# First layer of the first token tile's first column group in plain float32, with those weights' splits eight slots later

## The chip, the cores and the metric

The kernel runs on one core of a Trainium2 chip. The metric is the device time of one execution in microseconds (us). The kernel before took 508.42 us, the median of three runs (508.11 to 509.48).

## What is computed

Three blocks follow one another on 1536 tokens (2 batches of 768) with 512 features (8 heads of 64).

```python
# attention: local window of 16 keys each side, and 24 block summaries
k_sum = k.reshape(B, H, nb, 32, D).max(axis=3); v_sum = v.reshape(B, H, nb, 32, D).mean(axis=3)
scores_all = concat([where(mask_l, scale * q @ k.T, -1e9), scale * q @ k_sum.T + log(32)])
x = softmax(scores_all) @ concat([v, v_sum])          # 1536 x 512
# a two-layer block with 2048 hidden columns; w_in and w_out are float64
h = x @ w_in
g = where(h > 0, h, exp(min(h, 0)) - 1)
x = g @ w_out
# a routed block: 8 experts, argmax over x @ w_gate, relu(x @ w1[e]) @ w2[e], scaled by the gate
```

The change is in the second block and in its seam with the first.

## The kernel before, in words

The tokens are four tiles of 384 (`NT = 4`, `TT = 384`). The two-layer block runs over two groups of eight hidden column chunks of 128 (`NG = 2`, `FPG = 8`): for each group, for each tile t, for each chunk f, the first layer `mm1(t, f)` (line 387) makes `h` for 128 hidden columns and 384 tokens, the elu makes `g`, and the second layer `mm2(t, f)` (line 417) adds the chunk into three accumulators of 128 tokens.

**Precision.** Both layers work on split float32r values: a value is stored as a rounded copy and the rest (`x - rounded`), and a product is three matmuls (line 392). So `mm1` is 12 matmuls (4 chunks of 128 features times 3 passes). `xT[t]` holds both halves of the attention output: `act_o` (line 311, ScalarE) writes the rounded copy from PSUM, `dve_o` (line 317, VectorE) the rest; both read the PSUM bank "O".

**Weights.** `w_in` and `w_out` come as float64 words of 512 KB a chunk (`w_load`, 4 buffers). `w_conv` (line 359) makes float32 of one chunk with three VectorE instructions of 128x512 (lines 368, 372, 375). `w_split` (line 378) makes the two halves: a ScalarE copy (line 381) and a GpSimd subtraction (line 382). `i0` to `i7` are the chunks of `w_in`, `o0` to `o7` those of `w_out` of the first group. The weights of the second group are converted later and stored in HBM (`w_stash`), one per slot from slot 17 on. Splits are queued in `wpend` and done by `split_next`.

**Slots.** The order is written out by hand in one loop over slots `sl` (line 885); each engine runs its instructions in that order. Attention works in units of three query blocks, unit `u = sl` up to slot 17: scores `pe_s`, `dve_max` (line 272), `act_exp` (279), `norm` (lines 285, 286 on VectorE and 287 on GpSimd), `pe_t` (transposes, 294), `act_t`, `pe_o` (306), `act_o`. Units 0 to 7 make the first tile's x. From slot 18 on two units are done together in two slots. The two-layer block starts at slot `LAG = 9` with a running start: slot 8 has its own code (line 917) that does `mm1(0, 0)` and `mm1(0, 1)`, the first three feature chunks first and the last one when units 6 and 7 are done. Slot `9 + n` then does `mm1(0, n + 2)`, the elu of chunk n and `mm2(0, n - 1)`, up to n = 8. Slots 9 to 16 are called dense (line 1105); in them VectorE does `dve_max`, the elu's last step `elu_max` (line 404), one or two conversions interleaved with `norm`, and `dve_o`; GpSimd does the rest of `g` (`g_lo`, line 413), the splits and `norm`. From slot 17 on the second tile follows, chunk 0 first. `mm1` writes two PSUM banks in turn; a bank is free when `elu_max` has read it.

**Which weights when.** `corder` (line 834) converts, before the change, i0 in slots 5 and 6, i1 in 6 and 7, i2 in 7, o0 and i3 in 8, then o1 and i4 in 9, up to o4 and i7 in 12, o5 and o6 in 13 and o7 in 14. A split follows in the same slot (up to slot 8) or in the next.

Of the kernel before, what the change touches and what calls it, by code (L numbers as in the profile page):

```python
# [9 lines left out]
F32 = mybir.dt.float32  # L10
F32R = mybir.dt.float32r
BF16 = mybir.dt.bfloat16
I32 = mybir.dt.int32
U32 = mybir.dt.uint32
AF = mybir.ActivationFunctionType
ALU = mybir.AluOpType
# [4 lines left out]
P = 128  # L21
# [5 lines left out]
QB = 64  # L27
# [5 lines left out]
NCC = DM // P  # L33
# [4 lines left out]
TT = 384  # L38
# [11 lines left out]
def build(tc, cap, qT, kT, vT, vP, wi, wo, wg, wgT, wx, out):  # L50
# [6 lines left out]
    with ctx:  # L57
# [77 lines left out]
        mpool = px.enter_context(tc.tile_pool(name="mpool", bufs=2))  # L135

        xT = {}
        acc = {}
        W = {}

# [85 lines left out]
        def where(u):  # L226
            p, g = divmod(u, GPP)
            return p, p // NPAIR, p % NPAIR, g * GRP
# [81 lines left out]

        def act_o(u):
            p, t, pr, g0 = where(u)
            if pr == 0 and g0 == 0:
                xT[t] = xpool.tile([P, 2, NCC, TT], F32R, tag=f"xT{t}", name=f"xT{t}")
            nc.scalar.copy(xT[t][:, 0, pr, g0 * QB : (g0 + GRP) * QB], PS["o", u][:, 0 : GRP * QB])

        def dve_o(u):
            p, t, pr, g0 = where(u)
            q = slice(g0 * QB, (g0 + GRP) * QB)
            nc.vector.tensor_tensor(  # L320
                xT[t][:, 1, pr, q], PS.pop(("o", u))[:, 0 : GRP * QB], xT[t][:, 0, pr, q].bitcast(F32),
                op=ALU.subtract)
# [31 lines left out]
        def w_load(io, f):  # L354
            src = (wi if io == "i" else wo)[f].bitcast(U32)
            RW[io, f] = mpool.tile([P, 512, 2], U32, tag="raw", bufs=4, name=f"raw{io}{f}")
            nc.sync.dma_start(RW[io, f], src.rearrange("p (f two) -> p f two", two=2))

        def w_conv(which, parts=(0, 1, 2)):
            for part in parts:  # L360
                for io, f in which:
                    if part == 0:
                        raw = RW[io, f]
                        t = mpool.tile([P, 512], U32, tag="t1", bufs=T1, name=f"t1{io}{f}")
                        RW[io, f] = (raw[:, :, 0], raw[:, :, 1], t)
                    lo, hi, t = RW[io, f]
                    if part == 0:
                        nc.vector.tensor_scalar(
                            out=t, in0=hi, scalar1=3, scalar2=0x3FFFFFF8,
                            op0=ALU.logical_shift_left, op1=ALU.bitwise_and)  # L370
                    elif part == 1:
                        nc.vector.scalar_tensor_tensor(  # L372
                            out=t, in0=hi, scalar=0xC0000000, in1=t, op0=ALU.bitwise_and, op1=ALU.bitwise_or)
                    else:
                        nc.vector.scalar_tensor_tensor(  # L375
                            out=t, in0=lo, scalar=29, in1=t, op0=ALU.logical_shift_right, op1=ALU.bitwise_or)

        def w_split(io, f):
            src = RW.pop((io, f))[2].bitcast(F32)
            w = W[io, f] = wpool.tile([P, 2, 512], F32R, tag="W", name=f"W{io}{f}")  # L380
            nc.scalar.copy(w[:, 0], src)
            nc.gpsimd.tensor_tensor(w[:, 1], src, w[:, 0].bitcast(F32), op=ALU.subtract)  # L382

# [3 lines left out]
        def mm1(t, f, cs=range(NCC)):  # L387
            if cs[0] == 0:
                HP[t, f] = ph(f"h{t}_{f}")
            w = W["i", f]  # L390
            for c in cs:
                for n, (s, xs) in enumerate(((0, 0), (0, 1), (1, 0))):
                    nc.tensor.matmul(  # L393
                        HP[t, f][:, 0:TT], lhsT=w[:, s, c * P : (c + 1) * P], rhs=xT[t][:, xs, c, :],
                        start=c == 0 and n == 0, stop=c == NCC - 1 and n == 2)
# [228 lines left out]

        def alloc_expert(k):

            pl, tg = (wpool, "W") if k % 2 == 0 else (w2pool, "W2")
            EW[k] = [pl.tile([P, 2, 512], F32R, tag=tg, name=f"E{k}_{m}") for m in range(NCHUNK)]
            for i in range(k + 2, NE, 2):
                EW[i] = EW[k]  # L630

# [202 lines left out]
        corder = {}  # L834
        for f in range(NFC):
            if f < FPG:
                corder.setdefault(LAG - 4 + f, []).append(("i", f))
                corder.setdefault(LAG - 1 + f - (f > 5), []).insert(0, ("o", f))
            else:
                s0 = LAG + (NT - 1) * FPG + f % FPG  # L840
                corder.setdefault(s0, []).insert(0, ("i", f))
                corder.setdefault(s0 + 2, []).append(("o", f))
        order = [x for k_ in sorted(corder) for x in corder[k_]]
        nload = [0]


        later = order[2 * FPG :]
# [37 lines left out]
        for sl in range(total):  # L885
# [12 lines left out]
            if 0 <= n < FPG + 2:  # L898
                m1 = (0, 0, n + 2) if n + 2 < FPG else m1 if n >= FPG else None
                el = (0, 0, n) if 0 < n < FPG else el if n > FPG else None  # L900
                m2 = (0, 0, n - 1) if 0 <= n - 1 < FPG else None
            cv = list(corder.get(sl, ())) if sl >= LAG else []

            def conv_next():
                now = cv[:1]
# [11 lines left out]
            if sl == LAG - 1:  # L917

                pe_s(u)
                mm1(0, 0, range(NCC - 1))  # L920
                act_t(u - 2)
                w_split("i", 2)
                pe_o(u - 2)
                act_o(u - 2)
                w_conv([("o", 0)], (0, 1))
                dve_o(u - 2)
                pe_t(u - 1)
                mm1(0, 1, range(NCC - 1))
                w_conv([("o", 0)], (2,))
                w_prefetch()  # L930
                act_t(u - 1)
                pe_o(u - 1)
                w_split("o", 0)
                w_conv([("i", 3)], (0, 1))
                act_o(u - 1)
                dve_o(u - 1)
                mm1(0, 0, range(NCC - 1, NCC))
                mm1(0, 1, range(NCC - 1, NCC))
                w_conv([("i", 3)], (2,))
                w_prefetch()  # L940
                wpend.append(("i", 3))
                fin_va(p)
                load_vs(p)
                load_k(p + 2)
                dve_max(u)
                elu_exp(0, 0)
                elu_max(0, 0)
                act_exp(u)
                prep_k(p + 1)
                norm(u)  # L950
                g_hi(0, 0)
                g_lo(0, 0, nc.gpsimd)
                continue
# [182 lines left out]
            if dense:  # L1136
# [12 lines left out]
                w_conv(cv, (2,))  # L1149
                for x in cv:  # L1150
                    w_prefetch()
                wpend.extend(cv)
                cv = []
            if u < NU and sl % GPP == 0 and p + 1 < NPR:
                prep_k(p + 1)
            if u < NU and sl % GPP == 1 and p + 1 < NPR:
                if not dense:
                    prep_va(p + 1)
                if p + 2 < NPR:
                    load_vt(p + 2)  # L1160
            if sl == LAG - 3:
                w_conv([("i", 0)], (2,))
                w_prefetch()
                w_conv([("i", 1)], (0, 1))
            if sl == LAG - 2:
                w_conv([("i", 1)], (2,))
                w_prefetch()
            if sl < LAG and u - 2 in late:
                dve_o(u - 2)
            if u < NU and not dense:  # L1170
                norm(u)
            if sl in (LAG - 3, LAG - 2):
                w_split("i", sl - LAG + 3)
            if sl == LAG - 2:
                w_conv([("i", 2)])
                w_prefetch()
            if sl == LAG - 4:
                w_conv([("i", 0)], (0, 1))
            if sl >= LAG and u - 2 in late and not dense and u != NU:
                dve_o(u - 2)  # L1180
            if el and not dense:
# [286 lines left out]
```

## Time and profile before

| | |
|---|---|
| median of 3 runs | 508.42 us |
| the profiled execution | 508.64 us |
| its span | 506.9 us |
| TensorE matmuls busy | 472.0 us (93%), 3052 |
| weight loads busy | 406.9 us (80%) |
| VectorE busy | 325.6 us (64%) |
| ScalarE busy | 271.8 us (54%) |
| GpSimd busy | 189.3 us (37%) |
| granted TensorE clock, mean | 0.981 |

The profile is of one execution. PE is TensorE, PEld its weight loads, DVE VectorE, ACT ScalarE, POOL GpSimd, SP the engine that issues most DMAs. An instruction's duration includes what it waits for once it has started. Ends of matmuls are modelled, so a record is longer than the step to the next one. A clock of 1.00 is 2.4 GHz, 0.50 is 1.2 GHz.

### The profile page before, as it was taken

How to read it: one execution, taken by the hardware profiler on the slowest of the kernel's cores; microseconds unless marked ns; L12 is line 12 of the kernel's file. 1: busy time of each engine (PE TensorE's matmuls, PEld its weight loads, DVE VectorE, ACT ScalarE, POOL GpSimd, SP SyncE). 2: the span in 40 equal slices, each digit the busy share in tenths (PEclk: the TensorE clock that was granted, in tenths of full speed). 3: DMA queues.
4: the chain of work that ended last, by engine and by line, in shares of the span. 5: the costliest groups of instructions: out<-in, count | busy, mean ns of one | idle time of the engine just before them, and what ended most of it. 6: DMA issues, size and time to landing. Idle time of an engine off the chain costs nothing.

```text
span 506.9 us, 9236 instructions
## 1 busy us (share of the span) xinstructions
PE 472.0 (93%) x3052; PEld 406.9 (80%) x3052; DVE 325.6 (64%) x880; ACT 271.8 (54%) x681; POOL 189.3 (37%) x197
## 2 busy tenths in 40 slices
PE   7798798889999999999999999999998999999892
PEld 6586577678888889999999899888767989888672
DVE  4699999878877761111149889846686755556460
ACT  4755656666667646664333333334654865566550
POOL 4345575633333335883223233223335040030440
PEclk9988998999999999999999999999999999999997
DMA  8996656667777441439010010012645966458380
GB/s 237 283 255 185 191 162 189 214 207 245 227 230 219 126 142 46 125 118 345 37 62 2 0 63 0 2 63 88 200 129 151 345 211 222 135 164 278 105 292 15
DMA packets 45634, 79.97 MB, mean 158 GB/s; under 512 B 4604, under 2 KB 19196, under 8 KB 45552
## 3 DMA queue, kind: packets, MB, share of 16 engines
q1 hardware_dynamic: 43792, 73.83, 46.4%
q0 software_dynamic: 1760, 5.19, 3.4%
q8 instruction: 34, 0.56, 0.5%
q14 instruction: 48, 0.39, 0.2%
HBM read 65.29 MB, written 13.11 MB: 155 GB/s over the span
## 4 chain that ended last, share of the span: by engine, by line
PE 65%; DVE 15%; DMA 13%; issue 2%; ACT 2%; POOL 1%; SPq 0%; DVEq 0%; POOLq 0%
PE acc L426 23%; PE h L393 22%; DMA xgq<-x2d,gidx 10%; PE bh L750 6%; PE y L739 5%; DMA vt<-vT 2%; DVE t1i L375 2%; DVE t1i L372 2%; DVE t1o L375 1%; DMA xg<-x2d,gidx 1%; PE T L294 1%; DVE st L285 1%; DVE sc L272 1%; PE O L334 1%; DVE t1o L372 1%
## 5 line engine op out<-in xcount | busy, mean ns | idle before, releaser
L393 PE MATMUL h<-xT,Wi 128*128 128x384 f32 x768 | 152.8, 346 | 8.2 <-DVE e L404 6.6
L393 PEld LDWEIGHTS h<-xT,Wi 128*128 128x128 f32 x768 | 137.2, 192 | 16.5 <-DVE e L404 8.7
L426 PE MATMUL acc<-Wo,g 128*128 128x512 f32 x576 | 145.8, 397 | 1.0 <-POOL Wo L382 1.0
L413 POOL TENSOR_TENSOR g<-e,g 128x384 fp32r<-128x384 f32 x63 | 71.4, 1133 | 145.5 <-ACT g L409 129.9
L426 PEld LDWEIGHTS acc<-Wo,g 128*128 128x128 f32 x576 | 105.9, 188 | 21.7 <-POOL Wo L382 1.3
L404 DVE SCALAR_TENSOR_TENSOR e<-e,h 128x384 f32<-128x384 f32 x64 | 35.3, 551 | 77.3 <-ACT e L400 77.3
L399 ACT ACTIVATE e<-h 128x384 f32<-128x384 f32 x64 | 31.4, 491 | 65.4 <-PE h L393 61.8
L409 ACT CAST g<-e 128x384 fp32r<-128x384 f32 x64 | 32.8, 513 | 42.6 <-DVE e L404 42.6
L618 DVE TENSOR_TENSOR E<-rawq,E 128x512 fp32r<-128x512 f32 x70 | 46.7, 705 | 9.1 <-ACT E L608 8.0
L279 ACT ACTIVATE sc<-sc,st 128x120 f32<-128x120 f32 x96 | 36.8, 385 | 28.8 <-DVE st L272 28.6
L750 PE MATMUL bh<-xbq,E 128*128 128x256 f32 (+1 forms) x288 | 43.6, 303 | 2.7 <-ACT ysf L654 1.4
L608 ACT CAST E<-rawq 128x512 fp32r<-128x512 f32 x75 | 42.7, 617 | 6.2 <-DMA rawq<-wx 3.5
L750 PEld LDWEIGHTS bh<-xbq,E 128*128 128x128 f32 x288 | 41.3, 188 | 5.0 <-ACT ysf L654 1.6
L287 POOL TENSOR_TENSOR sc<-sc,st 128x360 f32<-128x360 f32 x32 | 29.6, 925 | 41.3 <-DVE st L286 20.1
L739 PE MATMUL y<-E,g 128*128 128x512 f32 x168 | 41.7, 393 | 0.0
L488 DVE CUSTOM_DVE_ANT_0 dot<-a,wgb 128x512 f32<-128x512 f32 x48 | 40.0, 887 | 0.0
L739 PEld LDWEIGHTS y<-E,g 128*128 128x128 f32 x168 | 30.6, 188 | 5.7
L400 ACT ACTIVATE e<-e 128x384 f32<-128x384 f32 x64 | 33.7, 526 | 2.0
L272 DVE CUSTOM_DVE_ANT_0 sc<-S,masks 128x120 f32<-128x120 f32 x96 | 21.5, 276 | 14.2 <-PE S L247 10.4
L758 DVE TENSOR_TENSOR g<-e,g 128x256 fp32r<-128x256 f32 (+1 forms) x24 | 11.3, 469 | 23.8 <-ACT g L757 23.6
L655 POOL DMA_INDIRECT out<-ys,sidx x6 | 6.3, 1053 | 47.4 <-ACT ys L654 46.0
L755 ACT ACTIVATE e<-bh 128x256 f32<-128x256 f32 (+1 forms) x24 | 10.1, 419 | 22.4 <-PE bh L750 22.4
(225 smaller groups left out, 634.5 us busy)
## 6 DMA issues: line engine op xcount, KB each, us to landing
rawq<-wx SPq DMA_DIRECT2D x88, 256.0 KB, 4.3
rawi<-wi SPq DMA_DIRECT2D x16, 512.0 KB, 5.0
rawo<-wo SPq DMA_DIRECT2D x16, 512.0 KB, 5.5
vw<-vP SPq DMA_DIRECT2D x16, 288.0 KB, 6.7
kt<-kT SPq DMA_DIRECT2D x8, 400.0 KB, 5.6
qt<-qT SPq DMA_DIRECT2D x16, 192.0 KB, 5.9
vt<-vT SPq DMA_DIRECT2D x8, 384.0 KB
out<-xg SPq DMA_DIRECT2D x12, 256.0 KB, 3.6
```

Source lines behind the costliest of these rows:

```text
L279: nc.scalar.activation(out=sc[:, gi], in_=sc[:, gi], func=AF.Exp, bias=st[:, 0, gi : gi + 1], scale=-1.0, accum_out=st[:, 1, gi : gi + 1])
L393: nc.tensor.matmul(HP[t, f][:, 0:TT], lhsT=w[:, s, c * P : (c + 1) * P], rhs=xT[t][:, xs, c, :], start=c == 0 and n == 0, stop=c == NCC - ...
L400: nc.scalar.activation(out=e, in_=e, func=AF.Relu, bias=1.0, scale=-1.0)
L404: nc.vector.scalar_tensor_tensor(out=e, in0=e, scalar=-1.0, in1=h[:, 0:TT], op0=ALU.mult, op1=ALU.max)
L409: nc.scalar.copy(gT[t, f][:, 0], EP[t, f])
L413: eng.tensor_tensor(g[:, 1], EP.pop((t, f)), g[:, 0].bitcast(F32), op=ALU.subtract)
L426: nc.tensor.matmul(accp[tb], lhsT=g[:, s, tb * P : (tb + 1) * P], rhs=w[:, ws], start=f % FPG == 0 and n == 0, stop=f % FPG == FPG - 1 and ...
L488: nc.vector.tensor_tensor_reduce(out=junk, in0=x2[t * BPT + tb], in1=WGB[e // 2][:, e % 2], scale=1.0, scalar=0.0, op0=ALU.mult, op1=ALU.a ...
L608: (nc.vector.tensor_copy if m in vec else nc.scalar.copy)(EW[k][m][:, 0], raw_of(k, m))
L618: (nc.gpsimd if m in pool else nc.vector).tensor_tensor(w[:, 1], raw, w[:, 0].bitcast(F32), op=ALU.subtract)
L739: nc.tensor.matmul(ys[b], lhsT=g[:, s, b * P : (b + 1) * P], rhs=w[:, ws], start=f == 0 and n == 0, stop=f == 7 and n == 2)
L750: nc.tensor.matmul(h[:, 0:nt], lhsT=EW[k][half * NCC + c][:, ws, fc * P : (fc + 1) * P], rhs=xb[:, s, c, 0:nt], start=n == 0, stop=n == 3 ...
```

## The change

For the first tile and the first group, `mm1` takes plain float32 operands: `act_o` writes the attention output as plain float32 into `X0`, `w_conv` writes the chunks i0 to i7 as plain float32 into `T0`, and `mm1(0, f)` for f below 8 is four plain float32 matmuls. `X0` and part of `T0` live in the buffer of the fourth tile's `xT`, the rest of `T0` in the homes of W i5 to i7. The split weights i0 to i7 are first needed by the second tile in slot 17; they are split from `T0`, queued one per slot in slots 16 to 23. `split_x0` makes the first tile's split xT, one feature chunk per slot in slots 20 to 23, for the second group. `dve_o` goes for the first tile. Each conversion of i0 to i7 runs about one slot later: i0 in slot 6, i1 in 7, i2 in 8 (with o0), then o1 and i3 in 9 up to o5 and i7 in 13, o6 in 14, o7 in 15. The split of o0 moves from slot 8 to slot 9. The split weights get one named buffer each instead of a pool of 16 in turn; expert 0's weights take the same buffers.

```diff
         def act_o(u):
             p, t, pr, g0 = where(u)
+            if t == 0:
+                if u == 0:
+                    x = xpool.tile([P, 2, NCC * TT], F32, tag=f"xT{NT - 1}", name="x0")
+                    X0.extend([x[:, 0].rearrange("p (c q) -> p c q", q=TT), x[:, 1].bitcast(U32)])
+                nc.scalar.copy(X0[0][:, pr, g0 * QB : (g0 + GRP) * QB], PS.pop(("o", u))[:, 0 : GRP * QB])
+                return
...
+        def split_x0(c):
+            if c == 0:
+                xT[0] = xpool.tile([P, 2, NCC, TT], F32R, tag="xT0", name="xT0")
+            x = X0[0][:, c]
+            nc.scalar.copy(xT[0][:, 0, c], x)
+            nc.vector.tensor_tensor(xT[0][:, 1, c], x, xT[0][:, 0, c].bitcast(F32), op=ALU.subtract)
+
         def dve_o(u):
             p, t, pr, g0 = where(u)
+            if t == 0:
+                return
...
+        def first_weights(f):
+            if not T0:
+                for a, last in ((0, 7), (2, 6), (4, 5)):
+                    w = wpool.tile([P, 2, 512], U32, tag=f"Wi{last}", bufs=1, name=f"T{a}")
+                    T0[a] = w[:, 0]
+                    T0[a + 1] = w[:, 1] if a < 4 else X0[1][:, 0:512]
+                T0[6], T0[7] = X0[1][:, 512:1024], X0[1][:, 1024:1536]
+            return T0[f]
...
-                        t = mpool.tile([P, 512], U32, tag="t1", bufs=T1, name=f"t1{io}{f}")
+                        if io == "i" and f < FPG:
+                            t = first_weights(f)
+                        else:
+                            t = mpool.tile([P, 512], U32, tag="t1", bufs=T1, name=f"t1{io}{f}")
...
-            w = W[io, f] = wpool.tile([P, 2, 512], F32R, tag="W", name=f"W{io}{f}")
+            w = W[io, f] = wpool.tile([P, 2, 512], F32R, tag=f"W{io}{f % FPG}", bufs=1, name=f"W{io}{f}")
...
         def mm1(t, f, cs=range(NCC)):
+            if t == 0 and f < FPG:
+                for c in cs:
+                    nc.tensor.matmul(
+                        HP[t, f][:, 0:TT], lhsT=T0[f][:, c * P : (c + 1) * P].bitcast(F32), rhs=X0[0][:, c],
+                        start=c == 0, stop=c == NCC - 1)
+                return
...
-                corder.setdefault(LAG - 4 + f, []).append(("i", f))
-                corder.setdefault(LAG - 1 + f - (f > 5), []).insert(0, ("o", f))
+                corder.setdefault(LAG - 3 + f, []).append(("i", f))
+                corder.setdefault(LAG - 1 + f, []).insert(0, ("o", f))
...
+            if FPG - 1 <= n < 2 * FPG - 1:
+                wpend.append(("i", n - FPG + 1))
+            if FPG + 3 <= n < FPG + 3 + NCC:
+                split_x0(n - FPG - 3)
...
                 mm1(0, 0, range(NCC - 1))
                 act_t(u - 2)
-                w_split("i", 2)
                 pe_o(u - 2)
                 act_o(u - 2)
-                w_conv([("o", 0)], (0, 1))
-                dve_o(u - 2)
+                w_conv([("i", 2)], (0, 1))
                 pe_t(u - 1)
                 mm1(0, 1, range(NCC - 1))
+                w_conv([("i", 2)], (2,))
+                w_prefetch()
+                w_conv([("o", 0)], (0, 1))
+                act_t(u - 1)
+                pe_o(u - 1)
+                act_o(u - 1)
                 w_conv([("o", 0)], (2,))
                 w_prefetch()
-                act_t(u - 1)
-                pe_o(u - 1)
-                w_split("o", 0)
-                w_conv([("i", 3)], (0, 1))
-                act_o(u - 1)
-                dve_o(u - 1)
+                wpend.append(("o", 0))
                 mm1(0, 0, range(NCC - 1, NCC))
                 mm1(0, 1, range(NCC - 1, NCC))
...
-                wpend.extend(cv)
+                    if x[0] == "o":
+                        wpend.append(x)
...
             if sl in (LAG - 3, LAG - 2):
-                w_split("i", sl - LAG + 3)
+                w_conv([("i", sl - LAG + 3)])
+                w_prefetch()
```

## Rows read from the trace of the kernel before

**Rows 1.** The page, chain that ended last, shares of the span by engine:

```profile
PE 65%; DVE 15%; DMA 13%; issue 2%; ACT 2%; POOL 1%; SPq 0%; DVEq 0%; POOLq 0%
```

**Rows 2.** Busy us (instructions) of each engine by stretch; clock, DMA share, GB/s last:

```profile
42.00:92.00 50.00, 41.98 (x300) 34.08 (x300) 48.86 (x110) 29.52 (x92) 31.52 (x24) 0.91 0.60 177
40.70:44.10 3.40, 3.35 (x18) 2.55 (x17) 2.90 (x10) 2.08 (x9) 1.05 (x1) 0.50 0.61 172
110.00:345.00 235.00, 234.73 (x1491) 208.59 (x1490) 138.69 (x403) 119.44 (x292) 90.50 (x82) 1.00 0.36 114
119.10:130.06 10.96, 10.96 (x102) 9.56 (x98) 9.73 (x29) 6.89 (x23) 3.86 (x4) 1.00 0.85 292
```

**Rows 3.** Groups of instructions, whole span: busy us, mean ns | idle before, releasers:

```profile
L393 PE MATMUL h<-xT,Wi 128*128 128x384 f32 x768 | 152.8, 346 | 8.2 <-DVE e L404 6.6 <-ACT xT L315 1.6
L426 PE MATMUL acc<-Wo,g 128*128 128x512 f32 x576 | 145.8, 397 | 1.0 <-POOL Wo L382 1.0
L258 PE MATMUL S<-kw,qt 64*64 64x120 f32 x216 | 16.0, 284 | 0.4 <-DVE st L272 0.3
L404 DVE SCALAR_TENSOR_TENSOR e<-e,h 128x384 f32<-128x384 f32 x64 | 35.3, 551 | 77.3 <-ACT e L400 77.3
```

**Rows 4.** VectorE in order of time, slot 11: start us, us, instruction:

```profile
59.61 0.27 DVE L272 CUSTOM_DVE_ANT_0 sc<-S,masks 128x120 f32<-128x120 f32 x1
...
61.67 0.68 DVE L372 SCALAR_TENSOR_TENSOR t1o<-rawo,t1o 128x512 uint32<-128x512 uint32 x1
62.27 1.50 DVE L372 SCALAR_TENSOR_TENSOR t1i<-rawi,t1i 128x512 uint32<-128x512 uint32 x1
63.69 1.24 DVE L285 TENSOR_SCALAR st<-st 128x3 f32<-128x3 f32 x1
...
65.06 1.62 DVE L375 SCALAR_TENSOR_TENSOR t1o<-rawo,t1o 128x512 uint32<-128x512 uint32 x1
66.61 1.27 DVE L375 SCALAR_TENSOR_TENSOR t1i<-rawi,t1i 128x512 uint32<-128x512 uint32 x1
67.80 0.27 DVE L272 CUSTOM_DVE_ANT_0 sc<-S,masks 128x120 f32<-128x120 f32 x1
```

**Rows 5.** GpSimd in order of time, slot 11, [idle before <- releaser]:

```profile
61.91 1.31 POOL L413 TENSOR_TENSOR g<-e,g 128x384 fp32r<-128x384 f32 x1 [2.92 <-issue]
63.18 1.72 POOL L382 TENSOR_TENSOR Wo<-t1o,Wo 128x512 fp32r<-128x512 f32 x1
64.86 1.27 POOL L382 TENSOR_TENSOR Wi<-t1i,Wi 128x512 fp32r<-128x512 f32 x1
66.09 1.24 POOL L287 TENSOR_TENSOR sc<-sc,st 128x360 f32<-128x360 f32 x1
```

**Rows 6.** TensorE in order of time, slot 8:

```profile
33.44 1.86 PE L393 MATMUL h<-xT,Wi 128*128 128x384 f32 x9
...
38.29 0.57 PE L306 MATMUL O<-pT,vw 120*64 120x64 f32 x12 [0.46 <-DVE xT L320]
40.48 2.43 PE L393 MATMUL h<-xT,Wi 128*128 128x384 f32 x6 [1.62 <-ACT xT L315]
```

**Rows 7.** TensorE in order of time, from slot 11 to slot 12:

```profile
64.55 0.50 PE L294 MATMUL T<-ident,sc 128*120 128x128 f32 x3
64.98 0.83 PE L258 MATMUL S<-kw,qt 64*64 64x120 f32 x12
...
69.01 2.35 PE L393 MATMUL h<-xT,Wi 128*128 128x384 f32 x12 [0.42 <-DVE e L404]
```

**Rows 8.** GpSimd in order of time, slots 14 and 15:

```profile
87.95 2.94 POOL L382 TENSOR_TENSOR Wo<-t1o,Wo 128x512 fp32r<-128x512 f32 x2
...
93.97 1.00 POOL L413 TENSOR_TENSOR g<-e,g 128x384 fp32r<-128x384 f32 x1 [2.32 <-issue]
```

**Rows 9.** VectorE in order of time, first scores of slot 15:

```profile
91.67 0.27 DVE L272 CUSTOM_DVE_ANT_0 sc<-S,masks 128x120 f32<-128x120 f32 x1
```

**Rows 10.** TensorE in order of time, first group of the second tile, slot 17:

```profile
101.37 2.27 PE L393 MATMUL h<-xT,Wi 128*128 128x384 f32 x12
```

More of the change, by code (lines that the diff above doesn't have):

```diff
@@ L137, in build @@
         xT = {}
+        X0 = []
+        T0 = {}
         acc = {}
@@ L625, in alloc_expert @@
         def alloc_expert(k):
-            pl, tg = (wpool, "W") if k % 2 == 0 else (w2pool, "W2")
-            EW[k] = [pl.tile([P, 2, 512], F32R, tag=tg, name=f"E{k}_{m}") for m in range(NCHUNK)]
+            if k % 2 == 0:
+                EW[k] = [
+                    wpool.tile([P, 2, 512], F32R, tag=f"W{io}{f}", bufs=1, name=f"E{k}_{m}")
+                    for m, (io, f) in enumerate(splits)]
+            else:
+                EW[k] = [w2pool.tile([P, 2, 512], F32R, tag="W2", name=f"E{k}_{m}") for m in range(NCHUNK)]
             for i in range(k + 2, NE, 2):
@@ L842, in build @@
                 corder.setdefault(s0 + 2, []).append(("o", f))
+        corder[LAG - 1].reverse()
         order = [x for k_ in sorted(corder) for x in corder[k_]]
         nload = [0]
+        splits = [("i", 0), ("i", 1)]
+        for f in range(2, FPG + 2):
+            splits += [x for x in (("i", f), ("o", f - 2)) if x[1] < FPG]
         later = order[2 * FPG :]
@@ L921, in build @@
                 act_t(u - 2)
-                w_split("i", 2)
                 pe_o(u - 2)
                 act_o(u - 2)
-                w_conv([("o", 0)], (0, 1))
-                dve_o(u - 2)
+                w_conv([("i", 2)], (0, 1))
                 pe_t(u - 1)
                 mm1(0, 1, range(NCC - 1))
+                w_conv([("i", 2)], (2,))
[4 more added lines that the diff above has]
+                act_o(u - 1)
                 w_conv([("o", 0)], (2,))
                 w_prefetch()
-                act_t(u - 1)
-                pe_o(u - 1)
-                w_split("o", 0)
-                w_conv([("i", 3)], (0, 1))
-                act_o(u - 1)
-                dve_o(u - 1)
+                wpend.append(("o", 0))
                 mm1(0, 0, range(NCC - 1, NCC))
                 mm1(0, 1, range(NCC - 1, NCC))
-                w_conv([("i", 3)], (2,))
-                w_prefetch()
-                wpend.append(("i", 3))
                 fin_va(p)
@@ L1160, in build @@
                     load_vt(p + 2)
[L1161 to L1167, printed above, removed]
             if sl < LAG and u - 2 in late:
@@ L1172, in build @@
             if sl in (LAG - 3, LAG - 2):
-                w_split("i", sl - LAG + 3)
-            if sl == LAG - 2:
-                w_conv([("i", 2)])
+                w_conv([("i", sl - LAG + 3)])
                 w_prefetch()
-            if sl == LAG - 4:
-                w_conv([("i", 0)], (0, 1))
             if sl >= LAG and u - 2 in late and not dense and u != NU:
```

## The prediction

> **What bounds the kernel now.** I read the chain that ended last first. It is 65% TensorE and 15% VectorE [rows 1], so the question is where each of the two rules. The busy time by stretch answers it [rows 2]: from 110 to 345 us TensorE is busy for 234.73 of 235.00 us, and whatever is gained before 110 us is kept only if TensorE reaches that stretch earlier. From 42 to 92 us it is the other way round: VectorE is busy 48.86 of 50.00 us, TensorE 41.98, and the clock granted to TensorE is 0.91 there, 0.50 (1.2 GHz) from 40.7 to 44.1 us: part of the time TensorE runs at half clock, and that costs little while VectorE is late. The groups of instructions say the same from TensorE's side [rows 3]: of 8.2 us that the matmuls of the first layer waited in all, 6.6 were for `e` of line 404, the VectorE step that frees their PSUM bank.
>
> One slot of that stretch shows why VectorE is late. Slot 11 runs from the first score row at 59.61 us to the next slot's at 67.80, 8.19 us [rows 4]. The same instruction on the same 128x512 tile (L372) takes 0.68 us and then 1.50; L285, which has three columns, takes 1.24. GpSimd's rows lie exactly beside them [rows 5]: L372 ends when `g` (L413) has ended, L285 ends with the Wo subtraction, L375 follows the end of the Wi subtraction, the last L375 that of L287. The two engines take turns, whole instruction by whole instruction: 1.27 us of this chain is the Wi subtraction.
>
> **The change, part by part.** The profiled execution took 508.64 us with a span of 506.9, 1.7 us around it; the median of the runs shown is 508.42, 0.2 less. Slots are numbered as in the loop.
>
> *Plain float32 matmuls.* A column group of the first tile had 12 float32r matmuls of 384 columns; it gets 4 plain ones. The trace has no plain product of 128x128 by 384. Plain products stand in it as two records each (L258 has 6 calls a slot and 12 records), with a mean of 284 ns for 120 columns; float32r has 346 for 384 and 397 for 512 [rows 3]. That is 0.40 ns a column, so 120 columns of float32r would have 346 - 264 x 0.40 = 240 ns; the plain record has 44 more, hence 0.77 ns a column. Nine float32r matmuls last 1.86 us at full clock [rows 6], 0.346 of it the last: eight steps of 0.19 us, 0.04 over their columns; twelve are 2.2 to 2.3. Eight plain records then cost 8 x (384 x 0.77 + 35 ns) = 2.6 us: 0.4 more per group, 3.2 for eight. Ends: 1.5 us if a plain record streams like float32r (8 x 0.19), 3.5 if the twelve records of L258 that last 0.83 us [rows 7] are two heads side by side (1.15 ns a column). I take 2.6, between them and from the recorded durations. It is covered in slots 10 to 13 only while VectorE is slower; uncovered it is the full 0.4.
>
> *Slot 8.* Before, the two first groups cannot finish until VectorE has emptied the output bank (a wait of 0.46 us) and ScalarE, which first stood behind a weight split, has stored the last xT (1.62 us); so the last column block starts at 40.48 us, at half clock, and ends at 42.91 [rows 6]. After, ScalarE alone empties the bank, no split stands in ScalarE's queue, and T0 needs only VectorE's three steps. From the start at 33.44: 6 records of 0.33, the output and transposes of about 0.95 us (from 35.2 to 36.0 with fill), 6 records, the last output and its copy 1.0, 4 records: 33.4 + 2.0 + 1.0 + 2.0 + 1.0 + 1.35 = 40.75 us. The first exp waits for the first of these two groups alone; its PSUM bank and the scores of slot 8 follow about 1.7 us earlier than now. VectorE has one weight conversion less before slot 9 (i3 moves into it) and no dve_o, so it isn't late. Gain 1.7 us, 0 if VectorE is late after all, 2.5 if not even that wait is left.
>
> *Slot 9.* o0's split takes the place of i3's on ScalarE and GpSimd: nothing.
>
> *Slots 10 to 13.* Each loses one Wi subtraction and one ScalarE copy. In slot 11, after the Wo subtraction (64.90 us), L285 and L286 run as now, then L375 at once (0.6) instead of after 66.13; L287 waits until that L375 ends (65.6), runs 0.8, and the second L375 0.5: 66.85 instead of 67.80. So 1.0 us, less than the 1.27 removed, since L287's turn is now waited for in the open. Four slots: 4.0 us. Bounds: 0 (L287 just takes the place) and 1.3 x 4 = 5.1. TensorE then has 4.04 us of other work between two first-layer groups (64.55 to 69.01, less the wait of 0.42) [rows 7] and 2.6 of its own, 6.65 of 7.2: still covered, and with so little idle time the half-clock stretches should go.
>
> *Slot 14.* It converted o7 beside two splits (2.94 us on GpSimd [rows 8]); now o6 beside one (half of that). L287 comes 1.3 us earlier and is out of the way of the slot's last VectorE copies: 0.6 us, between 0 and 1.3.
>
> *Slots 15 to 17 give back.* Now TensorE goes through them with hardly a wait: slot 15 begins at 91.67 on VectorE and the second tile's first group starts at 101.37, 9.7 us later [rows 9, 10]. After, slot 15 also converts o7 and slot 16 splits o7 and i0, and second-layer step f of the first tile waits for Wo f. In slot 15 GpSimd starts g 2.3 us after the slot's begin, as now (93.97 [rows 8]); g (1.0), a turn of L372 (0.6) and Wo6 (1.3) end at 5.2, and after the last turn of L375 VectorE closes the slot at 5.6. In slot 16 scores and elu (1.1), the exps and g's copy (1.6) put g at 8.3 to 9.3, Wo7 ends at 10.6, its nine matmuls take 2.2, and the first group of tile 1 starts at 12.8; Wi0 (11.9) is in time. Loss 3.1 us; 0 if GpSimd finds room beside VectorE's scores, 4.5 if Wi0 comes first.
>
> *Slots 17 to 23.* Seven more Wi splits and four split_x0 (a copy of 0.5 us and a subtraction of about 0.55 each, after L404's 551 ns for 384 columns [rows 3]) lie under the full TensorE; nothing, with the price in the third rival. Loads: the order of the raw loads shifts by one slot, each prefetch still two slots ahead of its use; SyncE's queue may be held some 2 us longer by the first one, ahead of q and v loads that are used two slots later: nothing.
>
> Sum: -1.7 - 4.0 - 0.6 + 3.1 = -3.2 us. 508.64 - 3.2 = 505.4, on the median's scale 505.2; I say 505.3.
>
> **The rivals.** (a) *The tail of the first tile gives nothing back*: Wo6 and Wo7 fit beside the scores, whose rows (0.27 us) aren't slowed beside GpSimd's end of L287 [rows 4, 5]. Against it: two GpSimd instructions more than now stand ahead of the second layer. Time: -6.3, 502.1.
>
> (b) *The turn is taken by the next one*: L287 or g holds VectorE as long as the Wi subtraction did, and slots 10 to 13 keep 8.2 us each. For it: every VectorE step from 62.27 on stands behind some GpSimd row [rows 4, 5]; against it, L287 is 0.8 us alone and was waited for already. Time: +0.8, 509.2.
>
> (c) *The moved subtractions come back in slots 18 to 23* (the slower side). VectorE is busy 9.73 of 10.96 us in a pair of slots there [rows 2], 1.23 idle. Two Wi subtractions of 1.27 may hold it 2.54 us, two split_x0 another 1.1. It decides once the added time passes the 1.23: 1.3 us in the first pair, 2.4 in each of the next two, 6.1 in all, 511.3. Against it: GpSimd is busy only 3.86 us of the pair, so that gaps are there, and scores that read PSUM take no turn. The Trainium skill speaks for this rival (SBUF — State Buffer, section "SBUF: two separate sides"): the port pair of the two engines is an exclusive lock that the first to start holds for its whole instruction, so a subtraction that is moved takes its hold along. The trace agrees on the hold: L285's 1.24 us [rows 4]; what it costs where TensorE rules no row shows.
>
> (d) *The plain matmuls cost 3.5 us*: 4.04 + 3.5 = 7.54 a slot, 0.3 over VectorE's 7.2 four times, and 1.8 more in slot 8. Time: +3.0 on the forecast, 508.3.
>
> **How the numbers follow.** My sum 0.52, (a) 0.15, (b) 0.12, (c) 0.13, (d) 0.08. About 0.3%, 1.5 us, is what a measurement here can tell from no change. Faster than 506.9 are nearly all of the sum's cases (0.49) and (a): 0.64. Within 0.3% lie (b), most of (d), and the sum's upper edge: 0.21. Slower: (c) and a worse (b): 0.15. The range leaves out the far half of (c) and the edge of (a): 501.8 to 509.3; the sum's own is 503.5 to 507.
>
> **What would show it.** Right: the first scores of slot 9 1.7 us earlier; slots 10 to 13 of 7.2 us, L285 and one L375 without a wait for Wi; eight records of L393 in about 2.6 us; the clock at full from 41 to 92 us; the second tile's first group at about 98 us, with waits of TensorE for Wo just before it; TensorE full from there. Wrong: slots of 8 us; a group of 3.5 us; waits for `e` of line 404 between 110 and 140 us.

## The result, and the profile after

The changed kernel takes 514.17 us, the median of five runs (510.33 to 516.87), against 508.42 for the kernel before in the same session (506.82 to 509.48). The ratio is 1.0104, 95% interval 1.0068 to 1.014: slower, and outside the range that was given. The profiled execution is the one of 514.17 us, with a span of 512.5, 5.6 more than before, and a mean granted clock of 0.988.

The first view is the busy time by stretch of the changed kernel. Columns: stretch, length, then busy us and instructions of PE, PEld, DVE, ACT and POOL, clock, DMA share, GB/s.

```profile
42.00:92.00 50.00, 44.58 (x308) 29.33 (x306) 47.67 (x112) 30.93 (x99) 27.20 (x21) 1.00 0.69 197
117.36:144.61 27.25, 23.09 (x200) 19.35 (x197) 24.21 (x62) 18.14 (x54) 13.31 (x13) 1.00 0.73 223
144.61:166.37 21.76, 21.76 (x197) 18.89 (x195) 16.93 (x57) 15.21 (x47) 7.81 (x9) 1.00 0.73 207
110.00:345.00 235.00, 230.84 (x1459) 204.73 (x1458) 142.54 (x400) 120.22 (x291) 96.00 (x85) 1.00 0.36 112
```

From 42 to 92 us it went as forecast: TensorE is busier than before (44.58 us against 41.98) and the clock is at 1.00, where it was 0.91 [rows 2]. But the stretch from 110 to 345 us, which TensorE filled before (234.73 of 235.00 us), now has 4.16 us of idle time, and all of it lies in slots 20 to 23: 27.25 us long, TensorE busy 23.09. The same four slots of the kernel before:

```profile
119.10:141.01 21.91, 21.91 (x198) 19.11 (x194) 17.98 (x56) 14.64 (x46) 7.89 (x9) 1.00 0.82 260
```

They are 5.34 us longer: 4.16 us of it is TensorE's idle time, the rest is busy time, mostly of runs that are now broken in two (the scores of a pair, 0.85 us before, are 0.42 and 0.83 us), whose ends are modelled. VectorE's busy time in them has grown by 6.23 us (17.98 to 24.21), GpSimd's by 5.42. Slots 24 to 27 take 21.76 us, as before.

The groups of instructions, as in [rows 3]: the plain product has its own line (L421), which stands twice because its tiles' buffers have different names. No first-layer matmul in split values (L428, second tile on) waits for anything. The scores of the paired units (L249) do.

```profile
L428 PE MATMUL h<-xT,Wi 128*128 128x384 f32 x672 | 129.8, 339 | 0.0
L421 PE MATMUL h<-x,T 128*128 128x384 f32 x40 | 14.4, 499 | 2.9 <-DVE e L439 2.5 <-ACT x L319 0.4
L421 PE MATMUL h<-x 128*128 128x384 f32 x24 | 8.5, 499 | 1.7 <-DVE e L439 1.7
L249 PE MATMUL S<-kw,qt 64*64 64x120 f32 x168 | 7.1, 273 | 2.4 <-DVE e L439 2.4
```

TensorE in slot 8, as in [rows 6]: six records for each of the first two groups, then the last column block of both at 41.31 us, ended at 42.87.

```profile
35.29 2.20 PE L421 MATMUL h<-x,T 128*128 128x384 f32 x6
...
38.30 2.10 PE L421 MATMUL h<-x,T 128*128 128x384 f32 x6
40.33 0.57 PE L308 MATMUL O<-pT,vw 120*64 120x64 f32 x12
41.31 1.56 PE L421 MATMUL h<-x,T 128*128 128x384 f32 x4 [0.42 <-ACT x L319]
...
43.95 2.85 PE L421 MATMUL h<-x,T 128*128 128x384 f32 x8 [0.32 <-DVE e L439]
```

VectorE and then GpSimd in slot 11, as in [rows 4, 5]: the slot lasts from 66.11 to 73.47 us, 7.36 instead of 8.19. After the turn of the Wo subtraction (L287, 1.23 us) the first L404 runs in 0.66, and no Wi subtraction stands before L289.

```profile
66.11 0.27 DVE L274 CUSTOM_DVE_ANT_0 sc<-S,masks 128x120 f32<-128x120 f32 x1
...
70.19 1.23 DVE L287 TENSOR_SCALAR st<-st 128x3 f32<-128x3 f32 x1
...
71.55 0.66 DVE L404 SCALAR_TENSOR_TENSOR t1o<-rawo,t1o 128x512 uint32<-128x512 uint32 x1
72.13 1.28 DVE L404 SCALAR_TENSOR_TENSOR x<-rawi,x 128x512 uint32<-128x512 uint32 x1
...
73.47 0.27 DVE L274 CUSTOM_DVE_ANT_0 sc<-S,masks 128x120 f32<-128x120 f32 x1
```

```profile
68.42 1.30 POOL L448 TENSOR_TENSOR g<-e,g 128x384 fp32r<-128x384 f32 x1 [2.78 <-issue]
69.68 1.71 POOL L411 TENSOR_TENSOR Wo<-t1o,Wo 128x512 fp32r<-128x512 f32 x1
71.80 1.06 POOL L289 TENSOR_TENSOR sc<-sc,st 128x360 f32<-128x360 f32 x1 [0.41 <-PE O L308]
```

TensorE at the end of the first tile, slots 16 and 17: a wait of 0.93 us for Wo6, one of 1.53 for the transposed scores of unit 15 (L300 on ScalarE), and the second tile's first group at 99.63.

```profile
92.21 2.11 PE L461 MATMUL acc<-Wo,g 128*128 128x512 f32 x8 [0.93 <-POOL Wo L411]
...
96.94 0.57 PE L308 MATMUL O<-pT,vw 120*64 120x64 f32 x12 [1.53 <-ACT pT L300]
97.44 2.35 PE L461 MATMUL acc<-Wo,g 128*128 128x512 f32 x9
99.63 0.69 PE L428 MATMUL h<-xT,Wi 128*128 128x384 f32 x3
```

The loss itself, TensorE from slot 20 to 22: in each pair of slots it waits once for the bank of the scores (0.88 and 0.80 us, L249 waiting for `e`) and once for ScalarE's copy pT (1.24, and 1.25 in the second pair).

```profile
118.65 0.83 PE L249 MATMUL S<-kw,qt 64*64 64x120 f32 x20 [0.88 <-DVE e L439]
...
127.64 0.52 PE L296 MATMUL T<-ident,sc 128*120 128x128 f32 x3 [1.24 <-ACT pT L300]
...
132.23 0.83 PE L249 MATMUL S<-kw,qt 64*64 64x120 f32 x20 [0.80 <-DVE e L439]
```

Why `e` is late stands in VectorE's rows from slot 19 to the begin of slot 20, beside GpSimd's Wi subtraction:

```profile
113.43 1.32 DVE L200 COPY kw<-ks 128x144 f32<-128x144 f32 x1
...
117.58 0.55 DVE L330 TENSOR_TENSOR xT<-x,xT 128x384 fp32r<-128x384 f32 x1
118.05 0.55 DVE L439 SCALAR_TENSOR_TENSOR e<-e,h 128x384 f32<-128x384 f32 x1
```

```profile
113.35 1.32 POOL L411 TENSOR_TENSOR Wi<-T,Wi 128x512 fp32r<-128x512 f32 x1
```

and the same two VectorE steps of the kernel before:

```profile
114.90 0.22 DVE L198 COPY kw<-ks 128x144 f32<-128x144 f32 x1
...
117.95 0.55 DVE L404 SCALAR_TENSOR_TENSOR e<-e,h 128x384 f32<-128x384 f32 x1
```

Slot 20 begins at 117.36 us after and at 119.10 before. So `e` starts 1.15 us before the slot's begin in the kernel before, and 0.69 after it in the changed one: 1.84 us later. Of this the copy that waits out the Wi subtraction makes 1.10 (1.32 for 0.22) and the new subtraction of split_x0 (L330) 0.5; the rest was there when the copy started. The first four of the 24 score records run at once; the next need the PSUM bank "S1", which `h` of the step before holds until L439 has read it.

The wait for pT comes by two ways. On VectorE a subtraction of split_x0 stands ahead of the next `e`; it takes 1.15 us beside GpSimd's L289 (123.70 to 124.76 us), where the one at 117.58 took 0.55. ScalarE's copy of `g` has to wait for that `e`, 1.57 us instead of 0.85 before. Behind it stand three more copies, Wi, kw and pT, of which Wi is new (0.52 us to the next one). The fourth, of split_x0, stands behind pT and costs nothing here: the next pT waits for TensorE anyway (0.28 us).

```profile
124.02 1.15 DVE L330 TENSOR_TENSOR xT<-x,xT 128x384 fp32r<-128x384 f32 x1
125.09 0.54 DVE L439 SCALAR_TENSOR_TENSOR e<-e,h 128x384 f32<-128x384 f32 x1
```

```profile
125.67 0.52 ACT L444 CAST g<-e 128x384 fp32r<-128x384 f32 x1 [1.57 <-DVE e L439]
126.09 0.61 ACT L410 CAST Wi<-x 128x512 fp32r<-128x512 f32 x1
126.61 0.51 ACT L197 COPY kw<-kt 128x384 f32<-128x384 f32 x1
127.02 0.47 ACT L300 COPY pT<-T 120x384 f32<-120x384 f32 x1
127.39 0.51 ACT L329 CAST xT<-x 128x384 fp32r<-128x384 f32 x1
128.19 0.48 ACT L300 COPY pT<-T 120x384 f32<-120x384 f32 x1 [0.28 <-PE T L296]
```

The copy of `g` in the kernel before, in the same place:

```profile
125.03 0.51 ACT L409 CAST g<-e 128x384 fp32r<-128x384 f32 x1 [0.85 <-DVE e L404]
```

### The profile page after: what moved, and what is told of

Same layout as the page of the kernel before. It is cut to its first block, busy times and chain, and to the rows that moved or that the text cites. A ratio compares the mean times of both kernels' runs of the same rounds, so it can differ in the third digit from the quotient of the medians.

```text
span 512.5 us, 9156 instructions
## 1 busy us (share of the span) xinstructions
PE 473.5 (92%) x3020; PEld 398.3 (78%) x3020; DVE 325.8 (64%) x876; ACT 272.8 (53%) x685; POOL 190.0 (37%) x197
## 5 line engine op out<-in xcount | busy, mean ns | idle before, releaser
L428 PE MATMUL h<-xT,Wi 128*128 128x384 f32 x672 | 129.8, 339 | 0.0
L428 PEld LDWEIGHTS h<-xT,Wi 128*128 128x128 f32 x672 | 118.0, 188 | 5.4 <-issue 1.5
L439 DVE SCALAR_TENSOR_TENSOR e<-e,h 128x384 f32<-128x384 f32 x64 | 35.3, 551 | 78.4 <-ACT e L435 78.4
L653 DVE TENSOR_TENSOR E<-rawq,E 128x512 fp32r<-128x512 f32 x70 | 48.2, 727 | 12.3 <-ACT E L643 11.5
L289 POOL TENSOR_TENSOR sc<-sc,st 128x360 f32<-128x360 f32 x32 | 29.5, 922 | 45.0 <-DVE st L288 32.8
L300 ACT COPY pT<-T 120x384 f32<-120x384 f32 x32 | 15.3, 478 | 14.3 <-PE T L296 12.6
```

Source lines behind the costliest of these rows:

```text
L428: nc.tensor.matmul(HP[t, f][:, 0:TT], lhsT=w[:, s, c * P : (c + 1) * P], rhs=xT[t][:, xs, c, :], start=c == 0 and n == 0, stop=c == NCC - ...
L439: nc.vector.scalar_tensor_tensor(out=e, in0=e, scalar=-1.0, in1=h[:, 0:TT], op0=ALU.mult, op1=ALU.max)
L653: (nc.gpsimd if m in pool else nc.vector).tensor_tensor(w[:, 1], raw, w[:, 0].bitcast(F32), op=ALU.subtract)
```

## The experiments

Runs of one session share the runs of the kernel before; ratios are to those. Times of stretches are read from TensorE's rows of each profile.

**Both kernels once more.**

> The changed kernel once more, unedited. Theory M (the moved subtractions and split_x0 come back in slots 18 to 23): TensorE's waits of about 5.3 us between its first group of tile 1 (slot 17) and slot 24 repeat to within 0.3 us, since they are made by the order of instructions. Rival R (the extra time comes from before 42 us, where the profile had a half-clock stretch of 6.8 us instead of 3.4 and a vt load 0.57 us later): the start of mm1(0,0), 35.29 us in the first profile against 33.44, is what varies from run to run, and the time goes with it.

Changed kernel: 513.94 us, before 509.83, ratio 1.0086 [1.0055, 1.0116]. The loss is there again; slots 20 to 23 took 26.13 us in this execution. The time up to the first first-layer group, 1.9 us longer in the first profile, is 0.1 shorter than before in this one. In the twelve profiles of changed versions that group starts anywhere from 31.46 to 38.03 us (33.44 and 34.03 in the two of the kernel before), so those 1.9 us aren't shown to be an effect of the change. From the second tile's first group to slot 20 this execution took 19.27 us instead of 17.72, with a stretch at half clock from 105 to 108 us (0.53); four of the twelve profiles have such a loss there, and why is not known.

> The kernel before, unedited, for a second profile. M: slots 20 to 23 take 21.9 us from the scores of slot 18's pair to those of slot 22's as in its first profile, the stretch from the last large expert to the first transposes of the small one (472 to 477 us) 4.3 us; the first 25 us vary by a few us from run to run, as they did between the profiles of the changed kernels (25.3 to 28.7 us). If instead the stretch at 472 us takes 6 to 7.5 us here as well, the 1.6 to 3.2 us that every changed kernel lost there have nothing to do with the change.

508.85 against 510.41, 0.9979 [0.9943, 1.0015]. Slots 20 to 23 took 21.91 us here too, to the hundredth.

**split_x0 moved out of slots 20 to 23**, to slots 24 and 25.

```diff
-            if FPG + 3 <= n < FPG + 3 + NCC:
-                split_x0(n - FPG - 3)
+            if n in (2 * FPG - 1, 2 * FPG):
+                for c in range(2):
+                    split_x0(2 * (n - 2 * FPG + 1) + c)
```

> split_x0 two chunks each in slots 24 and 25 instead of one each in slots 20 to 23. M: the waits of TensorE in slots 20 to 23 (5.3 us in the profile of the change) shrink to about 2.2, since 0.47 and 1.07 us of split_x0 stand directly ahead of line 404's step twice each; 3 us faster than the changed kernel, some 511. R: no change, 514.

512.39 us, 1.0048 [1.0019, 1.0077]. Slots 20 to 23: 23.37 us, 1.46 over the kernel before, with only the Wi splits in them. Slots 24 to 27: 23.22 instead of 21.76. Without split_x0 2.8 to 3.9 us of the loss are gone there, and in its new place, ahead of `elu_max` again, it costs 1.5 us. The copy L200 still takes 1.31 us beside the Wi subtraction.

**The Wi split behind prep_k and act_t**, in slots 19, 21 and 23.

```diff
-                split_next()
+                if even or n >= 2 * FPG:
+                    split_next()
...
                     act_t(a)
+                    if n < 2 * FPG:
+                        split_next()
```

> In slots 19, 21 and 23 the Wi split stands behind prep_k and behind act_t(a) instead of ahead of both; even slots and split_x0 as in the change. M: prep_k's last copy (1.3 us beside the Wi subtraction) is back at 0.2 and ScalarE's copy for the transposes comes 0.6 us earlier; the waits of slots 20 to 23 shrink from 5.3 to about 2.5 us, some 511. R: no change, 514.

512.46 us, 1.005 [1.0018, 1.0083]. Slots 20 to 23: 24.87, 2.4 less than in the first profile of the changed kernel and 1.3 less than in the second, with the same instructions in them. L200 takes 0.22 us again, and the two waits for pT are 0.71 and 0.74 us instead of 1.24 and 1.25: about 0.5 us each was the Wi copy, the rest comes by `e`.

**The deferral undone**: i2 to i7 are split one slot after their conversion, i0 and i1 in slots 6 and 7; the plain float32 product stays.

```diff
-            if FPG - 1 <= n < 2 * FPG - 1:
-                wpend.append(("i", n - FPG + 1))
...
-                wpend.append(("o", 0))
+                wpend.extend([("i", 2), ("o", 0)])
...
-                    if x[0] == "o":
-                        wpend.append(x)
+                    wpend.append(x)
...
+                w_split("i", sl - LAG + 3)
```

> Only the deferral undone: i0 and i1 split in slots 6 and 7, i2 to i7 one slot after their conversion; the plain float32 first groups and split_x0 stay. M: slots 10 to 13 take 8.2 to 8.4 us again instead of 7.2 (4 us back), slots 16 to 19 have no Wi subtraction; of the 5.3 us of waits in slots 20 to 23 the share of split_x0, about 3, stays; in sum about 1 us slower to 1 us faster than the change, 513 to 515. R (the deferral is worth its 4 us and costs nothing later): 4 us slower than the change, 518.

519.3 us, 1.0154 [1.0105, 1.0203], the slowest of all (4.6 us of its profile lie ahead of the first first-layer group, which is not explained). The first-layer groups of slots 10 to 13 are 8.2 us apart again, 32.70 us from that of slot 10 to that of slot 14 (33.12 before); so nearly all the gain of those slots is the moved split, and plain float32 by itself gains at most 0.4 us there. Slots 20 to 23, now with split_x0 and no Wi split, take 24.11 us, 2.2 over the kernel before: split_x0 alone is a cost in that place. Together with the Wi splits alone (1.46) that makes 3.7 us, less than the 4.2 and 5.3 of both at once.

**Both moves together** (split_x0 in slots 24 and 25, Wi splits behind act_t).

> split_x0 in slots 24 and 25, and in slots 19, 21 and 23 the Wi split behind prep_k and act_t(a). M: the stretch of slots 20 to 23, 26.1 to 27.3 us in the change, 23.4 and 24.9 with one edit alone, comes to 21.9 to 22.3; 4 to 5 us faster than the change, 509 to 510. Rival (the two edits take away the same waits): no better than the better one alone, 512.4.

511.71 us, 1.0021 [0.9996, 1.0046]. Slots 20 to 23 are 22.77 us, slots 24 to 27 23.39. Of 5.3 us, 2.5 are left, 1.6 of them where split_x0 now is.

**split_x0 in VectorE's gap.** VectorE waits in even slots between `g_lo` and the next scores (1.59 us in slot 20 and 1.05 in slot 22 of the kernel before). Two chunks in slot 20 and two in 22, ScalarE's copies behind `elu_exp`, the subtractions behind `g_lo`; Wi splits as in the run before.

```diff
                     elu_exp(*el[1:])
+                if n in (FPG + 3, FPG + 5):
+                    for c in range(2):
+                        split_x0(n - FPG - 3 + c, 0)
...
                         g_lo(*el[1:], nc.gpsimd)
+                if n in (FPG + 3, FPG + 5):
+                    for c in range(2):
+                        split_x0(n - FPG - 3 + c, 1)
```

> Slots 19, 21 and 23 split Wi behind prep_k and act_t(a), as in the version with both moves, but split_x0 stands in slots 20 and 22, two chunks in each: ScalarE's copies right behind elu_exp, VectorE's subtractions behind g_lo, where VectorE waits in the even slots. Theory (the loss of slots 20 to 23 is the place of the moved work in the queues): slots 20 and 21 stay near 22.8 us, slots 22 and 23 return from 23.4 to about 21.8 us; the execution is 1.6 us shorter than the version with both moves, near 510. Rival (the loss is the amount of work): slots 22 and 23 come to 21.8 but slots 20 and 21 grow to 24 or more, and the time is 511.7 or more.

(The expectation names slots wrongly: 22.8 us is the time of slots 20 to 23, and the 23.4 that was to become 21.8 that of slots 24 to 27.) 509.76 us against 510.04, ratio 1.0004 [0.9979, 1.0028]. By stretch, slots 20 to 23 and then 24 to 27, here from the output matmuls 0.8 us ahead of the scores (cut in this way, the kernel before takes 21.92 and 21.76 us):

```profile
115.30:138.20 22.90, 22.69 (x195) 19.32 (x194) 22.52 (x63) 17.46 (x53) 13.36 (x12) 1.00 0.80 247
138.20:160.00 21.80, 21.80 (x195) 18.92 (x194) 17.27 (x58) 15.19 (x47) 7.80 (x8) 1.00 0.74 220
```

All the moved work is in those four slots, VectorE is busy 22.52 of 22.90 us, and TensorE still 22.69. So nearly all of the work fits; it was its place that cost time. What is left over the kernel before is 1.0 us.

**The tail.** Three attempts on the 2.7 us that slots 16 and 17 give back. First, o7 converted one slot earlier, with o6, on top of both moves:

```diff
-                corder.setdefault(LAG - 1 + f, []).insert(0, ("o", f))
+                corder.setdefault(LAG - 1 + f - (f > 6), []).insert(0, ("o", f))
...
+        corder[LAG + FPG - 3].reverse()
```

> As late_both, and o7 converted in slot 14 with o6, instead of slot 15. M: the stretch from slot 14's last transposes to the second tile's first group, 11.2 us in every changed kernel and 8.5 before, falls to about 9.5, slot 14 grows from 6.55 to about 8.2 us; in sum 0 to 1 us faster than late_both. Rival (it is i0's split that makes the tail long): the stretch stays at 11 us and the sum is 1.5 us slower.

512.35 us, 1.0046 [1.0017, 1.0076]; slots 16 and 17 took 11.94 us instead of 11.16, so no gain is shown. In that execution a half-clock stretch from 88.9 to 92.3 us lies beside it, which the run does not separate from the move.

Second, o7's split ahead of `elu_exp` in slot 16, on top of split_x0 in the gap:

```diff
+            if n == FPG - 1:
+                split_next()
             if el:
                 elu_exp(*el[1:])
```

> The kernel beside it, and in slot 16 the split of o7 is issued ahead of elu_exp and dve_max, so that Wo7 should be done earlier. Theory: the last group of the tail waits for Wo7, and the stretch of slots 16 and 17 shortens from 11.2 to about 10.3 us, 0.85 us off the time. Rival (that stretch waits for act_t(15) and elu, not for Wo7): it stays at 11.2 or grows, since dve_max of slot 16 now comes later.

513.22 us, 1.0059 [1.0034, 1.0084], 3.5 us more than the kernel beside it. Slots 16 and 17 grew to 12.01 us: ScalarE waits 2.46 us at that copy for VectorE's conversion, with `elu_exp` and the exps behind it. That is 0.85 us; in its profile a half-clock stretch from 106.8 us follows, slots 17 and 18 take 1.4 us more, and 1.6 us more lie ahead of the first first-layer group.

Third, Wo7's copy between `elu_exp` and `act_exp`, and Wi0's copy behind act_t(15):

```diff
                 dve_max(u)
+                if n == FPG - 1:
+                    split_next()
                 act_exp(u)
...
-                split_next()
-                split_next()
+                if n != FPG - 1:
+                    split_next()
+                    split_next()
```

> The version with split_x0 in slots 20 and 22; in slot 16 ScalarE's copy of Wo7 stands between elu_exp and act_exp (so dve_max and elu_exp are not held up), and Wi0's copy moves from slot 16 to slot 17 behind act_t(15). Theory: act_t(15) comes about 0.6 us earlier (0.52 for Wi0's copy, 0.52 for Wo7's, less 0.38 for act_exp), and Wo7's subtraction ends near 94 instead of 96.2 us, so slots 16 and 17 shorten from 11.16 to about 10.5 us and the time by 0.6 us, to about 509. Rival (the tail is held by VectorE's conversion of o7, whatever ScalarE's order): it stays at 11.1 to 11.2 or grows.

508.42 us against 510.15, ratio 0.9976 [0.9947, 1.0005], the best of all versions, though the interval still holds no change. Slots 16 and 17: 10.50 us, as the theory had it; TensorE's wait of 1.53 us for pT is now 0.82, and Wo7's subtraction ends at 93.8 us:

```profile
95.07 0.57 PE L308 MATMUL O<-pT,vw 120*64 120x64 f32 x12 [0.82 <-ACT pT L300]
```

**A wait that nobody moved.** In the small routed block, at about 475 us, TensorE stops after five matmuls (in one version six) of a run of 18, in all ten profiles of changed versions without padding; in the two of the kernel before it doesn't. The changed kernel, then the one before:

```profile
475.99 1.41 PE L715 MATMUL bh<-E,xbq 128*128 128x512 f32 x5 [1.41 <-issue]
478.89 3.17 PE L715 MATMUL bh<-E,xbq 128*128 128x512 f32 x13 [1.49 <-issue]
```

```profile
472.36 4.45 PE L676 MATMUL bh<-E,xbq 128*128 128x512 f32 x18 [2.00 <-issue]
```

The changed program has 32 matmuls and 32 weight loads fewer, so everything behind them lies elsewhere in TensorE's code. Idle matmuls of 8 columns in slot 5, where TensorE waits anyway, shift it back; 32 on top of both moves, then 16 on top of the best version.

```diff
+            if sl == 5:
+                fill = pacc("fill")
+                for _ in range(32):
+                    nc.tensor.matmul(fill[:, 0:NE], lhsT=ones, rhs=cums[0], start=True, stop=True)
```

> The same, and 32 bf16 matmuls of 8 columns for nothing (their result is not used) in slot 5, where TensorE waits 2 to 3 us for v: TensorE's program is then as long again as before the change (it had lost 32 matmuls and 32 weight loads). Theory P: the wait without a releaser in the small expert's first matmuls (1.5 to 1.7 us behind the fifth, in all changed kernels and not before) hangs on where in TensorE's program the block stands; with the old length it goes, 1.6 to 3 us. Rival: it stays (DMA or run-to-run), nothing.

> The kernel beside it with 16 idle matmuls of 8 columns added in slot 5, where TensorE waits anyway: nothing else changes but the place of all later instructions in TensorE's program. Theory (the 1.6 us wait behind the fifth matmul of the small expert, at about 472 us, depends on where the code lies): it goes or moves to another branch, as it did with 32 such matmuls, where a wait of 2.87 us came up at 448 us instead; the time changes by anything from -1.7 to +1.2 us. Rival (the wait belongs to the data, a late transfer or token list): it stays at 1.4 to 1.7 us in the same place and the time stays within 0.3 us of the kernel beside it.

512.73 us, 1.0041 [1.0011, 1.007], and 511.63 us, 1.0018 [0.9992, 1.0044]. In both the run of 18 is whole again, and a wait some 27 us earlier, ahead of another group of matmuls, has grown from about 0.9 to 2.87 and 3.47 us. With 16 of them:

```profile
443.59 2.71 PE L791 MATMUL bh<-xbq,E 128*128 128x256 f32 x11 [3.47 <-issue]
...
470.60 4.44 PE L717 MATMUL bh<-E,xbq 128*128 128x512 f32 x18 [1.83 <-issue]
```

So the wait goes with the length of TensorE's program ahead of it, and not with the data, which the padding leaves alone. What it waits for is not shown. In the DMA view of the changed kernel, cut to 475.80 to 477.30 us, stands one transfer of the kind "instruction" on queue 8, 0.02 MB:

```profile
q8 instruction: 1, 0.02, 6.4%
```

6.4% of 16 engines over 1.50 us is 1.5 us; it begins at about 475.9 us, so it ends at about 477.4, where TensorE stops. But the kernel before has such a transfer as well, between 472.40 and 473.50 us, and its run of 18 goes on:

```profile
q8 instruction: 1, 0.02, 5.2%
```

The Trainium skill has a rule for such waits (Runtime: NRT & Kernel Launch, section "Instruction fetch mechanics"): code is fetched in blocks, and a taken branch to a target outside the loaded pages waits for a fetch. The trace has a transfer at the stop, but also one where nothing stops; no row names the engine whose code it is, and no row shows a branch. That the wait is one for code remains a guess.

## Why the prediction was wrong

**The step that failed is "Slots 17 to 23", priced at nothing.** It measured +5.3 us in the first profile and +4.2 in the second, in slots 20 to 23; from the second tile's first group to slot 20 the first profile took 17.72 us, before 17.73 (the second 19.27, beside its half-clock stretch). Had it stood at 5 instead of 0, the sum would have been about +1.8. The prediction had this as its rival (c), with 6.1 us and a chance of 0.13, and put two things against it. "GpSimd is busy only 3.86 us of the pair, so that gaps are there" is true and no argument: each engine runs its instructions in the order that is written out, and the Wi subtraction was queued to start just when prep_k's copies run. "Scores that read PSUM take no turn" is true as well (0.28 us at 119.67, beside GpSimd's `g` from 119.22 to 120.23), but it was not the scores that were hit: it was L200, from SBUF to SBUF, 0.22 to 1.32 us. The Trainium skill's rule (SBUF — State Buffer, section "SBUF: two separate sides") is that a GpSimd operation and a VectorE one in a two-port mode, or with two SBUF inputs, share a port pair, and that whichever starts first holds it for its whole instruction. The row agrees with the hold: the copy started 0.08 us after the subtraction and ended 0.08 after it; in which mode it ran no row shows.

Rival (c) had the place, and nearly the price: its 4.8 us for slots 20 to 23 measured 5.3 and 4.2, its 1.3 us for slots 18 and 19 measured nothing. Its condition, though, is not what decided. It was to decide when added time passes the idle time of VectorE, 1.23 us a pair. In the changed kernel VectorE is still idle for 3.04 of the 27.25 us while TensorE waits; with split_x0 in the gap it is busy 22.52 of 22.90 us, and the loss is 1.0 instead of 5.3. Only that last 1.0 is near what the condition gives there, 4.4 us of added time less 3.8 of idle time, 0.6 (before, cut in the same way, it is busy 18.12 of 21.92 us). So that (c)'s sum came near the loss was in part luck. What decides the rest is which instruction stands behind the moved one: `elu_max`, which frees a bank and releases ScalarE's copy of `g`, and pT, for which TensorE's next matmuls wait. ScalarE's part was not seen at all; the copies were counted at 0.5 us each, and what waits behind them was not asked.

**The wait at 475 us** is a second loss that the prediction did not have: +1.6 us in the first profile, and +3.2 in the second, where a half-clock stretch from 476.4 us lies beside it.

**What came as forecast.** *Slot 8*: from the first group to the scores of slot 9 7.52 us instead of 9.53, -2.0 for -1.7. *Slots 10 to 13*: 29.16 instead of 33.12 us from the group of slot 10 to that of slot 14, -3.96 for -4.0; undoing the deferral showed that it is the moved split, and VectorE's rows of slot 11 that it is its subtraction. *Slot 14*: -0.8 for -0.6. *Slots 15 to 17*: +2.7 for +3.1, by the waits for Wo6 and act_t(15); Wo7, which the forecast had last, is ready at 97.47 us, just as its matmuls begin (97.44). *Plain group*: 2.68 us to the next instruction (60.10 to 62.78 us), 2.85 to the end of the last of eight records, 2.6 forecast. *Slot 9* was priced at nothing and took 0.45 more on TensorE, but not on VectorE, for whose `e` TensorE waits there (1.57 us ahead of the group at 52.74, before 1.53): from VectorE's first `e` to the scores of slot 10 8.19 us, before 8.18. Counted at that `e` (43.34 us after, 43.06 before), slot 8 gave 1.57. Together -3.6 for the -3.2 of the sum. With 5.3, 1.6 and the 1.9 before the first group, which did not come back in the second profile, that makes +5.2 of the 5.6 us of span.

**Rivals (a), (b) and (d)** are out: the tail gave 2.7 us back, the turn was not taken by the next one, and a group of 2.85 us still lay under VectorE's slot. Two readings of the rows were loose: L372 ends 0.55 us after `g` and not with it (63.77 and 63.22 us), and for (a) the scores at 67.80 us do not lie beside L287, which ends at 67.33; that scores aren't slowed beside GpSimd the row at 119.67 us shows.

What stays open: in slots 20 to 23, the last 1.0 us with split_x0 in the gap; what the wait at 475 us is for; and why the padded versions are slower in the median (511.63 against 508.42) while the profiled execution with 16 of them took 505.94. No version was shown to beat the kernel before.

## What to carry to other kernels

Moving work under an engine that is full is not free because the other engines have idle time in sum: look up the instruction that will stand right behind it on its own queue, the one beside it on an engine that it takes turns with, and who waits for those. Put moved work where its engine waits for others, behind what frees a bank and not ahead of it; that was worth 4 to 5 us here (ratio to the kernel before 1.0004 instead of 1.0086 and 1.0104), with the same work in both. A rival that is priced above the whole gain deserves more than a sum of busy times before it is put at 13%.

## What the runs showed of the hardware

A plain float32 matmul of 128x128 by 384 is two records of 499 ns each in the mean; eight in a row end after 2.85 us, which makes a step of 0.34 us (2.85 less 0.50, over seven), where twelve float32r records of a whole product take 2.36 (L428, at 119.41 us of the same trace). Their weight loads take 189 ns in the mean, as the float32r ones do with 188.

A VectorE copy of 128x144 from SBUF to SBUF takes 0.22 us, and 1.30 to 1.32 when a GpSimd subtraction of 128x512 has started just ahead of it; moving that subtraction away gave the 0.22 back.

With 64 instructions fewer early in TensorE's program a wait of 1.5 us came up some 400 us later, and with half or all of them put back it went, and a shorter one in another place grew to 2.9 and 3.5 us. A wait of 1.5 us is 0.3% of this kernel's time, so a difference of that size between two kernels need not come from what was changed (an estimate: the padded versions did not get faster in the median).
